# Gated mix of two linear attentions: query factors over one denominator, per-bank copies and earlier loads for the third query pair

## The chip, the cores and the metric

The kernel runs on one core of a Trainium2 chip. The metric is the device time of one execution in microseconds (us). The engines are PE (TensorE, the matmuls; PEld is its weight loader), DVE (VectorE), ACT (ScalarE), POOL (GpSimd) and SP (SyncE, which issues the DMA transfers; SPq is its queue).

## The reference

Two linear attentions over the same 2048 rows of 576 features, with 32 heads of 18 features, are mixed by a gate.

```python
g = _sigmoid((x * gate_w).sum(-1, keepdims=True))
a = _A_ref(x, A_wqkv, A_wo)      # phi = elu-like map of q and k
b = _B_ref(x, B_wqkv, B_w_phi, B_wo)
return g * a + (1 - g) * b
# inside B, per head, q and k first times w_phi:
phi_q = concatenate([softmax(pq), softmax(-pq)])      # 36 features from 18
kv = einsum("bhsf,bhsd->bhfd", phi_k, v);  z = sum over s of phi_k
o = (phi_q @ kv) / (phi_q @ z + 1e-6)
```

The part that matters here is B's query side. With u0 = exp(pq - max) and u1 = exp(min - pq), s0 and s1 their sums over the 18 features of a head, and z0, z1 the two halves of z, the two halves of phi_q are u0/s0 and u1/s1, and the denominator is u0.z0/s0 + u1.z1/s1 + 1e-6. Every row and head thus needs two factors, f0 = (1-g)/(s0 * den) for u0 and f1 = (1-g)/(s1 * den) for u1.

## The kernel before, in words

Rows go in 16 tiles of 128, two at a time: eight pairs. Three passes over the pairs follow each other: A's keys and values, B's keys and values, then the queries of both. Products with the weights are one level of Strassen on 2x2 blocks (`strassen`, lines 549 to 590): seven products per pair, accumulated in PSUM. Every float32 value is split into a high and a low float32r part, and three matmuls make up one product.

The query pass is `q_units` (lines 1169 to 1197) for a pair's Strassen steps. Its accumulators are X, Y and Z. X is filled with the first product, copied into SBUF as c1 (`keep`, line 556, on ACT), then more products are added into the same X: s2 (copied as c2), s3 (copied as c3), and the product of block 22, which is read as it stands. So PE cannot begin the next product into X before ACT has copied the last. Y is added to c1 on DVE (line 570), which also sets free the buffer that Z takes. X, Y and Z are two-bank PSUM tiles (`pq_tile`, tag pq, two buffers), with 288 columns in each bank, except that X of the first two pairs is made of two separate one-bank tiles (tags tr and bk, line 1192), which are copied one by one. `softmax_exp` (line 689) makes u0 and u1 (buffers named uw; vo and st stand for them in the second pair), their sums `ss` and, with one DVE reciprocal of 128x64, `rs`. `norm_a` (line 1127) and `norm_b` (line 1148) then make the scaled features: `norm_b` multiplies u by z_b (zw, one of the two on POOL), reduces to `dd` (128x64), multiplies dd by rs on POOL, adds the two halves and EPS to `den`, takes its reciprocal on DVE, and forms the factors in rs (line 1160); `scale_ub` writes u times its factor into the block buffer `late` (on POOL for the first two pairs, on DVE later). `tr_units` (line 1199) transposes A's features (`tr<-ident,row`) and the scaled blocks (`tr<-ident,late`) on PE, and ACT copies them out as uT. `num` (line 1220) multiplies uT with kb, the folded key-value blocks of B, and its results (vo, at) are copied by ACT and split by DVE. `out_units` (line 1244) multiplies them with the output weights WO (`bk<-op,vo`, `bk<-op,at`, `bk<-tail,at`) and stores the rows.

`fold_b` (line 1102) writes z_b and, by twelve small transfers on SP's queue (line 1124, 36 partitions of two or three runs of 18 numbers), kb. `x_fetch` (line 528) issues a pair's seven loads: xu, x1, xv, x2 (t2), then xp (s2 and s1), x3 (s3), x4 (s4, d), most of them into single buffers that the pair before still reads. The third query pair (n == 2 in `q_units`) has its loads issued in the loop's turn i == 1 (line 1302).

What sets the order of the work: the program is first recorded as a list of operations (`Plan`), each with its engine, its cost by a small formula and a due time worked backwards from the operations that need it (`order`, line 240); `run` (line 277) then picks, engine by engine, the ready operation that is due first. The order of each engine is so fixed when the program is built. All instructions carry the line of the call in `emit` (360; 365 in the changed kernel), so in the profile they are told apart by the names of their tiles.

## Time and profile before

| | us |
|---|---|
| median of 3 runs (lowest, highest) | 545.13 (544.47, 549.06) |
| the profiled execution, its own time | 544.94 |
| its span, first to last instruction | 543.2 |
| PE busy | 537.2 |
| DVE, ACT, POOL busy | 408.2, 291.1, 256.4 |
| granted TensorE clock | 0.999 |

How to read it: a row of the timeline gives the start in us, the duration of the group in us (first start to last end), engine, operation, out<-in, shapes, and how often; in brackets stands the idle time before it and what ended that. Matmul ends are modelled, so a group of matmuls seems to overlap the next: the pace is read from the starts of groups that follow each other. PEld's gaps show a wait of PE more fully than PE's own, for the same reason. A row of the windows view gives, for a stretch, the busy time of each engine, then the granted clock, the DMA share and GB/s.

### The profile page before, as it was taken

How to read it: one execution, taken by the hardware profiler on the slowest of the kernel's cores; microseconds unless marked ns; L12 is line 12 of the kernel's file. 1: busy time of each engine (PE TensorE's matmuls, PEld its weight loads, DVE VectorE, ACT ScalarE, POOL GpSimd, SP SyncE). 2: the span in 40 equal slices, each digit the busy share in tenths (PEclk: the TensorE clock that was granted, in tenths of full speed). 3: DMA queues.
4: the chain of work that ended last, by engine and by line, in shares of the span. 5: the costliest groups of instructions: out<-in, count | busy, mean ns of one | idle time of the engine just before them, and what ended most of it. 6: DMA issues, size and time to landing. Idle time of an engine off the chain costs nothing.

```text
span 543.2 us, 12968 instructions
## 1 busy us (share of the span) xinstructions
PE 537.2 (99%) x5233; PEld 518.6 (95%) x5233; DVE 408.2 (75%) x610; ACT 291.1 (54%) x612; POOL 256.4 (47%) x238
## 2 busy tenths in 40 slices
PE   9999999999999999999999999999999999999997
PEld 8999999999999999999999799999999999999997
DVE  5885587852798899989779989569598695976910
ACT  6865786645555645543376665354453544635430
POOL 5785486541884534363348685134252342523300
PEclk9999999999999999999999999999999999999999
DMA  8838767967759768768774831132231322200101
GB/s 288 321 127 268 270 242 273 344 219 305 277 220 339 250 201 280 237 210 261 290 268 147 347 98 59 57 116 71 81 101 59 110 72 81 70 24 1 45 23 43
DMA packets 40404, 96.38 MB, mean 177 GB/s; under 512 B 5460, under 2 KB 10068, under 8 KB 38808
## 3 DMA queue, kind: packets, MB, share of 16 engines
q1 hardware_dynamic: 40344, 95.56, 50.8%
q8 instruction: 41, 0.67, 0.5%
q14 instruction: 19, 0.16, 0.1%
HBM read 59.64 MB, written 36.70 MB: 177 GB/s over the span
## 4 chain that ended last, share of the span: by engine, by line
PE 96%; DMA 3%; DVE 0%; SPq 0%; issue 0%
PE pq L360 39%; PE bk L360 28%; PE tr L360 28%; DMA op<-wod 2%; DMA x<-s1x 1%; DVE row L360 0%; DVE dd L360 0%; SPq L360 0%; DVE epsc L360 0%
## 5 line engine op out<-in xcount | busy, mean ns | idle before, releaser
L360 PE MATMUL pq<-op,x 128*128 128x288 f32 (+1 forms) x624 | 102.3, 298 | 0.7 <-ACT row L360 0.7
L360 PEld LDWEIGHTS pq<-op,x 128*128 128x128 f32 x624 | 88.8, 188 | 1.5 <-ACT row L360 1.0
L360 PE MATMUL bk<-op,vo 128*128 128x288 f32 x480 | 70.7, 296 | 0.0
L360 PE MATMUL pq<-tail,x 128*128 128x288 f32 (+1 forms) x304 | 66.8, 299 | 0.3 <-DVE row L360 0.3
L360 PEld LDWEIGHTS bk<-op,vo 128*128 128x128 f32 x480 | 65.8, 188 | 0.0
L360 POOL TENSOR_TENSOR row<-row,z_a 128x576 f32<-128x576 f32 x16 | 25.8, 1609 | 60.1 <-issue 35.7
L360 PE MATMUL pq<-op,xp 128*128 128x288 f32 (+1 forms) x336 | 53.6, 297 | 0.1
L360 PE MATMUL bk<-op,at 128*128 128x288 f32 x288 | 51.0, 302 | 0.0
L360 PEld LDWEIGHTS pq<-tail,x 128*128 128x128 f32 x304 | 49.0, 188 | 1.5 <-issue 0.6
L360 POOL TENSOR_TENSOR row<-row,den 128x378 f32<-128x378 f32 (+1 forms) x32 | 23.8, 763 | 53.0 <-DVE den L360 53.0
L360 PEld LDWEIGHTS pq<-op,xp 128*128 128x128 f32 x336 | 47.4, 189 | 0.4 <-ACT row L360 0.4
L360 ACT ACTIVATE uT<-tr 118x512 f32<-118x512 f32 (+1 forms) x48 | 26.4, 561 | 39.1 <-PE tr L360 39.1
L360 ACT ACTIVATE row<-tr 128x288 f32<-128x288 f32 (+1 forms) x74 | 30.1, 408 | 29.8 <-PE tr L360 28.7
L360 ACT ACTIVATE row<-row,epsc 128x576 f32<-128x576 f32 x54 | 41.8, 774 | 3.3 <-DVE row L360 2.7
L360 PEld LDWEIGHTS bk<-op,at 128*128 128x128 f32 x288 | 41.5, 189 | 0.4 <-issue 0.4
L360 DVE TENSOR_REDUCE ss<-uw 128x64 f32<-128x1152 f32 x22 | 29.6, 1347 | 14.3 <-ACT uw L360 14.3
L360 POOL TENSOR_TENSOR x<-at,x 128x384 fp32r<-128x384 f32 (+2 forms) x35 | 32.0, 918 | 16.8 <-ACT x L360 14.9
L360 DVE TENSOR_TENSOR row<-row,pq 128x576 f32<-128x576 f32 (+1 forms) x30 | 22.2, 739 | 22.2 <-ACT row L360 15.5
L360 ACT ACTIVATE row<-bk 128x288 f32<-128x288 f32 (+2 forms) x42 | 17.2, 410 | 35.5 <-PE bk L360 35.3
L360 PE MATMUL tr<-op,xp 128*128 128x290 f32 (+1 forms) x216 | 33.4, 298 | 0.0
L360 ACT ACTIVATE uw<-uw 128x1152 f32<-128x1152 f32 x22 | 25.6, 1165 | 11.0 <-POOL uw L360 6.9
L360 PEld LDWEIGHTS tr<-op,xp 128*128 128x128 f32 x216 | 30.3, 189 | 0.2
(214 smaller groups left out, 1253.1 us busy)
## 6 DMA issues: line engine op xcount, KB each, us to landing
xp<-s0x SPq DMA_DIRECT2D x12, 512.0 KB
at<-xT SPq DMA_DIRECT2D x16, 320.0 KB
x<-x1x SPq DMA_DIRECT2D x12, 384.0 KB
x<-s2x SPq DMA_DIRECT2D x12, 384.0 KB
s0x<-xp SPq DMA_DIRECT2D x8, 512.0 KB
out<-row SPq DMA_DIRECT2D x14, 288.0 KB
op<-wb SPq DMA_DIRECT2D x3, 1152.0 KB
wod<-op SPq DMA_DIRECT2D x3, 1152.0 KB
```

The costliest lines, as they stand in the source:

```text
L360: fn(*[a.real() if isinstance(a, View) else a for a in args], **{k: v.real() if isinstance(v, View) else v for k, v in kw.items()})
```

## The change

There are three edits, and the planner's new order that follows from them.

1. B's query factors. For queries, `softmax_exp` returns the sums ss and takes no reciprocal of them. The factors are written over one denominator: with d0 = u0.z0 and d1 = u1.z1, f0 = (1-g) * s1 / (d0*s1 + d1*s0) and f1 = (1-g) * s0 / (d0*s1 + d1*s0). `norm_b` so multiplies dd on POOL by ss with its two halves swapped, adds the halves, takes the one reciprocal of 128x32, and forms the factors in dd. The 1e-6 has moved into z_b, as half of it per feature in each half (a bias of the ACT copy in `fold_b`). Sixteen DVE reciprocals of 128x64 go away, two per pair.
2. The third pair's X and Z are two-bank tiles that the planner tracks by bank: ACT copies c1, c2 and c3 in two instructions of 288 columns instead of one of 576, and the adds of Z are made in two.
3. The due times of the third pair's loads are set 15 us earlier (`plan.head = 15000`), so that the planner puts them between the transfers into kb.

```diff
     def cells(self):
 
         if self.tile.psum:
-            return np.zeros(1, np.int32)
+            return np.unique(self.idx[0] // 512).astype(np.int32) if self.tile.split else np.zeros(1, np.int32)
         if self.tile.dram:
             return self.idx.reshape(-1)
         n = math.prod(self.tile.shape[1:])
...
             op = Op()
             op.i, op.eng, op.calls, op.deps, op.succ, op.tiles = len(self.ops), eng, [], set(), [], set()
             op.cost, op.lag, op.lock, op.mode, op.dma = 0, 0, False, False, 0
+            op.head = self.head
             self.ops.append(op)
             if self.group is not None:
                 self.group.append(op)
...
             if op.eng != "PE":
                 after = [ops[s].due for s in (*op.succ, *frees.get(op.i, ()))]
                 op.due = min(after + [op.due + 60000]) - op.cost - op.lag - self.SEM
+        for op in ops:
+            if op.eng != "PE":
+                op.due -= op.head
         return self.run(tags)
 
     def run(self, tags):
...
     def tr_tile():
         return ps.tile([P, 512], F32, name="tr")
 
+    def halves_tile():
+        t = pq_tile()
+        t.tile.split = True
+        return t
+
     def two_banks(make=None):
         return [(make or tr_tile)() for _ in range(2)]
 
...
         if isinstance(acc, View):
             return [(slice(0, 2), acc)]
         return [(slice(a, a + 1), t[:, None]) for a, t in enumerate(acc)]
+
+    def by_half(acc):
+        return isinstance(acc, View) and acc.tile.split
 
     def half(acc, hf):
         return acc[:, hf] if isinstance(acc, View) else acc[hf]
...
     def tail_steps(x, w):
         return [(x(0, 0), w), (x(1, 0), w)]
 
-    def strassen(x, W, T, n, x_tile, c1_tile, c11, c22, c21, c12):
+    def strassen(x, W, T, n, x_tile, c1_tile, c11, c22, c21, c12, z_tile=pq_tile):
 
 
         def mul(acc, steps, start):
...
                 mm(acc, hf, n, steps, start, True)
 
         def keep(dst, acc, w):
+            if by_half(acc):
+                for a in range(2):
+                    A.activation(dst[:, a], acc[:, a, :w], AF.Copy)
+                return
             for a, t in parts(acc):
                 A.activation(dst[:, a], t[:, :, :w], AF.Copy)
 
...
         c2 = row_tile()[:, :D].rearrange("p (a c) -> p a c", a=2)
         keep(c2, X, HB)
         yield
-        Z = pq_tile()
+        Z = z_tile()
         mul(Z, tail_steps(x["t2"], T[:, 1]) + op_steps(x["s1"], W[5]), True)
         yield
         mul(X, op_steps(x["s3"], W[7]), False)
...
             V.scalar_tensor_tensor(fv[:, a], t[:, :, :HB], EPS, fv[:, a], op0=ALU.max, op1=ALU.add)
         return f
 
-    def softmax_exp(q, uw, eng=V):
+    def softmax_exp(q, uw, eng=V, inv=True):
         mm_ = sm.tile([P, 64], F32, name="mm")
         V.tensor_reduce(mm_[:, :32], heads(q), op=ALU.max, axis=AX.X)
         V.tensor_reduce(mm_[:, 32:], heads(q), op=ALU.min, axis=AX.X)
...
         A.activation(uw, uw, AF.Exp)
         ss = sm.tile([P, 64], F32, name="ss")
         V.tensor_reduce(ss, uw.rearrange("p s (h d) -> p (s h) d", d=DH), op=ALU.add, axis=AX.X)
+        if not inv:
+            return uw, ss
         rs = sm.tile([P, 64], F32, name="rs")
         V.reciprocal(rs, ss)
         return uw, rs
...
             pz = bank_tile()
             PE.matmul(pz[:, :36 * nh], sel[:, q], KB[:, :36 * nh], start=True, stop=True)
             A.activation(z_b[:, :, QH * DH * q:QH * DH * q + DH * nh].rearrange("p s (j d) -> p j s d", d=DH),
-                         pz[:, :36 * nh].rearrange("p (j s d) -> p j s d", s=2, d=DH), AF.Copy)
+                         pz[:, :36 * nh].rearrange("p (j s d) -> p j s d", s=2, d=DH), AF.Copy, bias=EPS / 2)
         pt = bank_tile()
         for m in range(3):
             PE.transpose(pt[:108, P * m:P * m + P], KB[:, 108 * m:108 * m + 108], ident)
...
         A.activation(ub[:, UB * 10 + 72:UB * NB], f2[:, 484:530], AF.Copy)
         return f2
 
-    def norm_b(t, uw, rs, ub, engs):
+    def norm_b(t, uw, ss, ub, engs):
         dd = sm.tile([P, 64], F32, name="dd")
         for s in range(2):
             zw = row_tile()[:, :D]
             engs[s].tensor_tensor(zw, uw[:, s, :], z_b[:, s], op=ALU.mult)
             V.tensor_reduce(dd[:, 32 * s:32 * s + 32], zw.rearrange("p (h d) -> p h d", d=DH),
                             op=ALU.add, axis=AX.X)
-        G.tensor_tensor(dd, dd, rs, op=ALU.mult)
+        swap = ss.rearrange("p (s h) -> p s h", s=2)[:, ::-1]
+        d2 = dd.rearrange("p (s h) -> p s h", s=2)
+        G.tensor_tensor(d2, d2, swap, op=ALU.mult)
         den = sm.tile([P, 32], F32, name="den")
-        V.scalar_tensor_tensor(den, dd[:, :32], EPS, dd[:, 32:], op0=ALU.add, op1=ALU.add)
+        V.tensor_tensor(den, dd[:, :32], dd[:, 32:], op=ALU.add)
         V.reciprocal(den, den)
-        r2 = rs.rearrange("p (s h) -> p s h", s=2)
-        V.scalar_tensor_tensor(r2, den[:, None, :].to_broadcast([P, 2, 32]), gate[:, 1, at_row(t):at_row(t) + 1], r2, op0=ALU.mult, op1=ALU.mult)
-        scale_ub(ub, uw, rs, engs[2])
+        V.scalar_tensor_tensor(d2, den[:, None, :].to_broadcast([P, 2, 32]), gate[:, 1, at_row(t):at_row(t) + 1], swap, op0=ALU.mult, op1=ALU.mult)
+        scale_ub(ub, uw, dd, engs[2])
 
     qs, norms = {}, []
     pairs = [NT // 2 - 2, NT // 2 - 1, *range(NT // 2 - 2)]
...
         qa, qb = {}, {}
 
         def c11(c):
-            qb[t1] = softmax_exp(c, uws[0], G)
+            qb[t1] = softmax_exp(c, uws[0], G, False)
+
+        def add(c, Z):
+            for a in ([slice(a, a + 1) for a in range(2)] if by_half(Z) else [slice(0, 2)]):
+                V.tensor_tensor(c[:, a], c[:, a], Z[:, a, :HB], op=ALU.add)
 
         def c22(c, Z):
-            V.tensor_tensor(c, c, Z[:, :, :HB], op=ALU.add)
+            add(c, Z)
             qa[t2] = phi_elu(c)
 
         def c21(X):
-            qb[t2] = softmax_exp(whole(X, uws[1]), uws[1])
+            qb[t2] = softmax_exp(whole(X, uws[1]), uws[1], V, False)
 
         def c12(c, Z):
-            V.tensor_tensor(c, c, Z[:, :, :HB], op=ALU.add)
+            add(c, Z)
             qa[t1] = phi_elu(c)
 
         def norm(t):
...
             qs[t] = (norm_a(t, qa[t], ub), ub)
             norm_b(t, *qb[t], ub, (G, V, G if t < 4 else V))
 
-        x_tile = (two_banks, lambda: two_banks(bank_tile))[n] if n < 2 else pq_tile
-        for i, _ in enumerate(strassen(x, WQ, TQ, HB, x_tile, c1_tile, c11, c22, c21, c12)):
+        x_tile = (two_banks, lambda: two_banks(bank_tile))[n] if n < 2 else halves_tile if n == 2 else pq_tile
+        for i, _ in enumerate(strassen(x, WQ, TQ, HB, x_tile, c1_tile, c11, c22, c21, c12, halves_tile if n == 2 else pq_tile)):
             if i in then:
                 then[i]()
             yield
...
         if i and i <= NT // 2:
             prev["ot"] = num(uT, prev["at"], i >= NT // 2 - 1)
         if i + 1 < NT // 2:
+            plan.head = 15000 if i == 1 else 0
             x = x_fetch(pairs[i + 1])
+            plan.head = 0
             if i == 0:
                 load_out(3, x["dma"])
                 load_out(4, x["dma"])
```

`cells` decides what the planner takes for one place in a tile; the lines left out only declare the new fields.

Where instructions move, first on SP, at the transfers into kb (the names x_ with a number are loads into x1, x2, x3 and x4). Before:

```order
L360 DMA kb<-row 36x3x18 x2
L360 DMA kb<-row 36x2x18
L360 DMA xu<-x0x_181 128x512
L360 DMA xp<-s0x_1972 128x1024
L360 DMA x_4206<-s1x_1992 128x512
L360 DMA op<-mad 2x2x1152
L360 DMA tail<-mad 2x1152
L360 DMA op<-wod 128x2304
L360 DMA xv<-x2x_231 128x512
```

and now, with the rows of the first two kb transfers ahead of it the same:

```order
L365 DMA xu<-x0x_181 128x512
L365 DMA kb<-row 36x2x18
L365 DMA kb<-row 36x3x18 x2
L365 DMA kb<-row 36x2x18
L365 DMA kb<-row 36x3x18
L365 DMA xp<-s0x_1972 128x1024
L365 DMA kb<-row 36x3x18
L365 DMA kb<-row 36x2x18
L365 DMA x_4167<-s1x_1992 128x512
L365 DMA kb<-row 36x3x18 x2
L365 DMA kb<-row 36x2x18
L365 DMA xv<-x2x_231 128x512
```

Three of the third pair's loads (xu, xp and s1x) now stand between the kb transfers, and xv ahead of the loads of the output weights.

On POOL, at the two `norm_b` of the first pair, from the first dd to the subtractions of the second pair's softmax (vo is that pair's u). Before:

```order
L360 TENSOR_TENSOR dd<-dd,rs 128x64
L360 TENSOR_TENSOR late<-uw,rs 128x10x3x18 x2
L360 TENSOR_TENSOR late<-uw,rs 128x2x2x18
L360 TENSOR_TENSOR dd<-dd,rs 128x64
L360 TENSOR_TENSOR row<-row,den 128x3x126
L360 TENSOR_TENSOR row<-row,den 128x198
L360 TENSOR_TENSOR late<-uw,rs 128x10x3x18 x2
L360 TENSOR_TENSOR late<-uw,rs 128x2x2x18
L360 TENSOR_TENSOR vo<-mm,row 128x576
L360 TENSOR_TENSOR vo<-row,mm 128x576
```

and now:

```order
L365 TENSOR_TENSOR dd<-dd,ss 128x64
L365 TENSOR_TENSOR late<-uw,dd 128x10x3x18 x2
L365 TENSOR_TENSOR late<-uw,dd 128x2x2x18
L365 TENSOR_TENSOR dd<-dd,ss 128x64
L365 TENSOR_TENSOR row<-row,den 128x3x126
L365 TENSOR_TENSOR row<-row,den 128x198
L365 TENSOR_TENSOR vo<-mm,row 128x576
L365 TENSOR_TENSOR late<-uw,dd 128x10x3x18 x2
L365 TENSOR_TENSOR late<-uw,dd 128x2x2x18
L365 TENSOR_TENSOR row<-row,z_a 128x576
L365 TENSOR_TENSOR vo<-row,mm 128x576
```

The subtraction vo<-mm,row now stands ahead of the second group of late, and the product with z_a ahead of the other subtraction.

On PE, at the third pair's X: s2 is `pq<-op,xp x12`, s3 the `pq<-op,x x12` behind it, block 22 `pq<-op,xv`; Z begins with `pq<-tail,x`. Before:

```order
L360 MATMUL bk<-op,at 128x288 x6
L360 MATMUL bk<-tail,at 128x288 x3
L360 MATMUL bk<-op,vo 128x288 x2
L360 MATMUL pq<-op,xp 128x288 x12
L360 MATMUL pq<-op,x_4206 128x288 x12
L360 MATMUL pq<-tail,x_3962 128x288 x2
L360 MATMUL pq<-op,xp 128x288 x6
L360 MATMUL pq<-tail,x_3962 128x288 x2
L360 MATMUL pq<-op,xp 128x288 x6
```

and now:

```order
L365 MATMUL pq<-op,x_4045 128x288 x6
L365 MATMUL pq<-tail,x_4045 128x288 x2
L365 MATMUL bk<-op,vo 128x288 x2
L365 MATMUL pq<-op,xp 128x288 x12
L365 MATMUL pq<-op,x_4167 128x288 x12
L365 MATMUL pq<-op,xv 128x288
L365 MATMUL pq<-tail,x_3962 128x288 x2
L365 MATMUL pq<-op,xp 128x288 x6
L365 MATMUL pq<-tail,x_3962 128x288 x2
L365 MATMUL pq<-op,xp 128x288 x6
L365 MATMUL pq<-op,xv 128x288 x5
```

One matmul of block 22 has moved ahead of Z, and the output product with at (six and three) is no longer there: it stands some 40 matmuls earlier, between the first product into X and the first group of late.

On DVE, what leads up to the addition of Y to c1, which is `row<-row,pq 128x576` here. Before:

```order
L360 RECIPROCAL rs<-ss 128x64
L360 SCALAR_TENSOR_TENSOR row<-row 128x576
L360 RECIPROCAL den<-den 128x32
L360 TENSOR_REDUCE ss<-st 128x64
L360 TENSOR_REDUCE dd<-row 128x32
L360 RECIPROCAL rs<-ss 128x64
L360 TENSOR_TENSOR at<-bk,at 64x256
L360 TENSOR_TENSOR row<-vo,z_b 128x576
L360 TENSOR_REDUCE dd<-row 128x32 x2
L360 TENSOR_TENSOR row<-row,pq 128x576
L360 TENSOR_TENSOR row<-st,z_b 128x576
```

and now:

```order
L365 TENSOR_REDUCE den<-row 128x32
L365 TENSOR_TENSOR row<-st,z_b 128x576
L365 TENSOR_REDUCE dd<-row 128x32
L365 RECIPROCAL den<-den 128x32
L365 TENSOR_REDUCE ss<-vo 128x64
L365 TENSOR_REDUCE dd<-row 128x32
L365 TENSOR_REDUCE ss<-st 128x64
L365 TENSOR_TENSOR row<-vo,z_b 128x576
L365 TENSOR_REDUCE dd<-row 128x32 x2
L365 TENSOR_TENSOR row<-row,pq 128x576
L365 TENSOR_TENSOR den<-dd 128x32
L365 RECIPROCAL den<-den 128x32
```

The two reciprocals of ss are gone, the product of st with z_b has moved from behind the addition to the head of the list, and at<-bk and the row<-row of phi have moved away from it.

More of the change, by code (lines that the diff above doesn't have):

```diff
@@ L118, in __init__ @@
         self.ops = 0
+        self.split = False
     def view(self):
@@ L136 @@
 class Op:
-    __slots__ = ("i", "eng", "calls", "deps", "succ", "tiles", "cost", "lag", "lock", "mode", "dma", "due", "left", "est", "key")
+    __slots__ = ("i", "eng", "calls", "deps", "succ", "tiles", "cost", "lag", "lock", "mode", "dma", "head", "due", "left", "est", "key")
 class Engine:
@@ L151, in __init__ @@
     def __init__(self):
-        self.ops, self.tiles, self.group, self.first = [], [], None, ()
+        self.ops, self.tiles, self.group, self.first, self.head = [], [], None, (), 0
     @contextmanager
```

## The prediction

> **What bounds the kernel now.** I read the page's busy times first, then PE's idle time by stretches, then the weight loader's timeline where it lies.
>
> ```profile
> span 543.2 us, 12968 instructions
> ...
> PE 537.2 (99%) x5233; PEld 518.6 (95%) x5233; DVE 408.2 (75%) x610; ACT 291.1 (54%) x612; POOL 256.4 (47%) x238
> ```
>
> PE is busy for all but 6.0 us, and the change takes no matmul away, so it can only win idle time of PE. The windows view (the stretch, its length, then busy us of PE, PEld, DVE, ACT and POOL) shows where that is:
>
> ```profile
> 0.00:295.00 295.00, 293.75 (x3369) 286.52 (x3370) 229.47 (x314) 175.91 (x374) 160.66 (x147) 1.00 0.74 255
> 295.00:315.00 20.00, 18.51 (x137) 16.33 (x135) 19.23 (x30) 12.06 (x24) 14.91 (x16) 1.00 0.84 324
> 315.00:520.00 205.00, 205.00 (x1583) 197.34 (x1582) 157.12 (x263) 99.44 (x207) 80.83 (x77) 1.00 0.21 68
> 520.00:543.20 23.20, 19.94 (x151) 18.43 (x150) 2.40 (x5) 3.72 (x9) 0.00 (x0) 0.99 0.11 39
> ```
>
> 1.25 us are the start and 3.26 us the last copy and store; neither is touched. The other 1.5 us lie between 295 and 315 us, where the second query pair ends and the third begins and DVE is busy for 19.23 of 20 us. From 315 us on PE waits for nobody: what is won before stays won, and DVE time saved later is worth nothing. Since PE's ends are modelled, the weight loader shows the waits more fully:
>
> ```profile
> 295.86 0.69 PEld L360 LDWEIGHTS pq<-op,xu 128*128 128x128 f32 x5 [0.52 <-DVE mm L360]
> ...
> 305.56 1.62 PEld L360 LDWEIGHTS pq<-op,xp 128*128 128x128 f32 x12 [0.36 <-ACT row L360]
> 308.16 1.62 PEld L360 LDWEIGHTS pq<-op,x 128*128 128x128 f32 x12 [0.97 <-ACT row L360]
> 310.32 0.30 PEld L360 LDWEIGHTS pq<-tail,x 128*128 128x128 f32 x2 [0.54 <-DVE row L360]
> ```
>
> Four waits, 0.52 + 0.36 + 0.97 + 0.54 = 2.4 us: the most that the change can win. That is 0.44%, under the 1% that a measurement of this kernel can tell from no change.
>
> The chain of waits puts the last of them down to a load, which is wrong:
>
> ```profile
> 294.02 5.71 DMA x<-s1x
> ...
> 300.17 8.65 DMA op<-wod
> ...
> 308.87 0.74 DVE dd L360
> ```
>
> The reduction at 308.87 is the second of two on a DVE that never paused (rows below); the weights only happen to land 0.05 us earlier. DVE's own queue sets that wait.
>
> **Part by part: the first wait.** The loader's row blames DVE, but PE's own row says that it was the load of xu:
>
> ```profile
> 282.69 10.21 SPq L360 DMA_DIRECT2D kb<-row  x12
> 293.00 0.46 SPq L360 DMA_DIRECT2D xu<-x0x  x1
> ```
>
> ```profile
> 282.04 1.86 PE L360 MATMUL bk<-op,xu 128*128 128x288 f32 x12
> ...
> 295.89 0.90 PE L360 MATMUL pq<-op,xu 128*128 128x288 f32 x5 [0.31 <-DMA xu<-x0x]
> ...
> 299.65 1.95 PE L360 MATMUL tr<-uT,kb 118*64 118x256 f32 x16
> ...
> 303.82 0.95 PE L360 MATMUL bk<-op,at 128*128 128x288 f32 x6
> 304.61 0.56 PE L360 MATMUL bk<-tail,at 128*128 128x288 f32 x3
> ```
>
> The kb issues take 0.85 us each on SP; xu goes out behind all twelve and is used 2.9 us later. Now it stands behind two, at about 282.7 + 1.7 = 284.4, and lands near 287.3; its buffer's last read by the second pair, the group from 282.04, is over by then. So the 0.5 us go, and PE begins the third pair at 295.4. The three loads put between push the last kb issue from about 292.1 to 293.3, or 294 if xp waits a little for PE. PE first reads kb at 299.65, which covers this: even if a kb transfer took the 5.7 us of s1x above, it would land just in time.
>
> **The second wait.** The first product's X has to be copied as c1 before s2 goes into it. ACT comes to that late; from the last uT copy on its queue is full:
>
> ```profile
> 298.87 0.49 ACT L360 ACTIVATE uT<-tr 118x384 f32<-118x384 f32 x1
> 299.24 1.17 ACT L360 ACTIVATE vo<-vo 128x1152 f32<-128x1152 f32 x1
> ...
> 304.87 0.64 ACT L360 ACTIVATE row<-pq 128x576 f32<-128x576 f32 x1
> 307.45 0.65 ACT L360 ACTIVATE row<-pq 128x576 f32<-128x576 f32 x1 [1.94 <-PE pq L360]
> 308.70 0.21 ACT L360 ACTIVATE row<-row 128x6 f32<-128x6 f32 x1 [0.60 <-POOL row L360]
> ```
>
> 299.24 to 305.51 is 6.3 us of work without a pause. The new order has the same ACT work between uT and c1, so the question is when that uT copy is made. It hangs on the second group of late, which POOL writes:
>
> ```profile
> 289.15 2.57 POOL L360 TENSOR_TENSOR late<-uw,rs 128x540 f32<-128x540 f32 x3 [1.50 <-DVE rs L360]
> ...
> 292.00 1.31 POOL L360 TENSOR_TENSOR row<-row,den 128x378 f32<-128x378 f32 x2
> 293.67 2.56 POOL L360 TENSOR_TENSOR late<-uw,rs 128x540 f32<-128x540 f32 x3 [0.36 <-DVE rs L360]
> 296.18 1.17 POOL L360 TENSOR_TENSOR vo<-mm,row 128x576 f32<-128x576 f32 x1
> ```
>
> Now vo<-mm,row is ahead of that group. The first group starts about 0.2 later (DVE has moved a dd and the split of at ahead of its factors, but lost two reciprocals), so POOL reaches vo<-mm,row at 293.5, and 293.5 + 1.17 + 2.56 gives 297.2: 1.0 us later than 296.2. PE meanwhile does 12 matmuls on xu and four of the output product: 295.4 + 16 x 0.132 = 297.5 (0.132 us from the six at 303.82). It just does not wait. Eleven transposes and five matmuls later, about 299.5, the last uT copy can start; it ends at 300.1. ACT's 6.3 us, less the second bank's share of 0.6, put the first bank of c1 at 305.8. So **s2 starts at 305.8 instead of 305.56**: what the early load won is lost again in ACT's queue, and this wait grows to about 1.2.
>
> **The split's own price**, from the groups of this pass:
>
> ```profile
> L360 ACT ACTIVATE row<-bk 128x288 f32<-128x288 f32 x33 | 13.5, 408 | 23.2 <-PE bk L360 23.1
> ...
> L360 ACT ACTIVATE row<-pq 128x576 f32<-128x576 f32 x18 | 11.7, 651 | 14.6 <-PE pq L360 14.6
> ```
>
> 2 x 408 against 651 ns: +0.17 us, three times, 0.5 on an ACT that sits idle for 0.6 and 1.9 us beside the copies of c2 and c3. Z's two added DVE instructions come behind the point that counts.
>
> **The third wait.** Whole, c2 is copied from 307.45 on, when both banks are done, and s3 waits until 308.16. By bank, s2's first half ends at 305.8 + 0.8 and 0.3 for the pipeline (307.45 against the 307.15 that 305.56 + 1.6 gives), and its copy ends at 307.3, while PE does the second half until 307.4. ACT has the row<-row of 308.70 and two late copies ahead of it, 0.6 us, which wait for POOL until about 306.2 (four products behind the exponential of st, below: 301.9 + 1.4 + 0.8 + 1.4 + 0.6 by POOL's rows for the same); that ends near 307.2. So **s3 starts at 307.4 instead of 308.16, a net 0.75**.
>
> **The fourth wait.** Z takes Y's buffer when DVE has added Y to c1 (the row at 309.53):
>
> ```profile
> 300.44 1.35 DVE L360 TENSOR_REDUCE ss<-vo 128x64 f32<-128x1152 f32 x1 [0.68 <-ACT vo L360]
> ...
> 303.04 0.55 DVE L360 RECIPROCAL rs<-ss 128x64 f32<-128x64 f32 x1
> 303.50 0.70 DVE L360 SCALAR_TENSOR_TENSOR row<-row 128x576 f32<-128x576 f32 x1
> ...
> 306.23 0.54 DVE L360 RECIPROCAL rs<-ss 128x64 f32<-128x64 f32 x1
> 306.69 0.35 DVE L360 TENSOR_TENSOR at<-bk,at 64x256 fp32r<-64x256 f32 x1
> 306.97 1.32 DVE L360 TENSOR_TENSOR row<-vo,z_b 128x576 f32<-128x576 f32 x1
> 308.21 1.40 DVE L360 TENSOR_REDUCE dd<-row 128x32 f32<-128x576 f32 x2
> 309.53 0.74 DVE L360 TENSOR_TENSOR row<-row,pq 128x576 f32<-128x576 f32 x1
> ```
>
> 303.04 to the start of the next instruction, 310.19, is 7.15 us. The two reciprocals go (2 x 0.46 by the distance of starts), row<-row (0.6) and at<-bk (0.3) have moved away; row<-st,z_b (0.7), one more dd (0.65) and ss<-vo (1.27) have moved in: 7.9 us. It would be 7.4 if row<-vo,z_b ran at its 0.7 instead of 1.24, without POOL beside it. The new list begins with row<-st,z_b, which needs the exponential of st: that is the second item of ACT's queue after 300.1, behind one of 0.7, so done at 301.9. The addition ends at 309.3 to 309.8 against 310.19. PE has finished s3 and one more matmul at 309.15 and waits again, 0.3 to 0.8. Z starts at 309.45 to 310.0 with one matmul (0.13) more behind it: a gain of 0.45 to 1.0 us. **I take 0.8**, since POOL's product with vo has moved forward and meets DVE's less.
>
> Behind that, the subtraction of vo on DVE, which PE's next transposes need, is by the same sums 0.3 us ahead of PE. The other twelve reciprocals go from turns in which PE waits for nothing. The 1e-6 in the z_b copies, the swapped halves and tensor_tensor for scalar_tensor_tensor replace instructions one for one: nothing.
>
> The sum, against the profiled execution: 544.94 - 0.8 = **544.1 us**. That execution lies 0.2 under the median of the runs shown, well inside their spread, so the forecast stays.
>
> **The rivals.**
>
> *All of the wait goes* (0.17): 544.94 - 2.4 = 542.5. For it: each wait has an edit aimed at it. Against it: ACT would have to reach c1 1.2 us, and DVE the addition 1.5 us, before the times above.
>
> *Nothing moves* (0.20): if a matmul into the first bank waits for both copies after all, s3 starts at 308.1, and with DVE at its late end 0 to 0.4 are left: 544.5 to 544.9. Against it: the first two pairs keep X in two tiles, and no wait of PE shows at their s3.
>
> *Slower, from POOL* (0.15). The place is the second group of late, only 0.3 ahead of PE. The 297.2 uses undisturbed durations; beside DVE the same shape of instruction takes longer:
>
> ```profile
> 414.90 1.64 POOL L360 TENSOR_TENSOR uw<-mm,row 128x576 f32<-128x576 f32 x1
> ```
>
> 1.64 against the 1.17 of vo<-mm,row is 0.5 us. Two or three such stretches put the end of late at 298.2 to 298.7; then PE, uT, ACT's exponentials and DVE's list follow it one for one. From 298.0 the 0.8 is eaten; at 298.7, with row<-vo,z_b slow as well, the time is 545.6. Against it: DVE is in reductions for half of that time. The Trainium skill (SBUF — State Buffer, "Who interferes with whom") says that a DVE instruction with two SBUF inputs contends with a GpSimd instruction that reads SBUF, and that a reduction never does. The two durations agree with it. By that rule vo<-mm,row would not be stretched where it now stands, beside reductions, and the time would be the forecast's 544.1.
>
> **How the numbers follow.** The forecast has 0.48. All four cases lie between 542.5 and 545.6, inside the 1% (539.7 to 550.6), so same has 0.96; 0.02 on either side are for a wait in the later turns, which would count several times. The range takes both end cases in, with a little for the spread of a median: 542.4 to 546.0.
>
> **What would show it.** Right: PE at the first pq<-op,xu without a wait, near 295.4; s2's wait for ACT grown from 0.36 to about 1.2, s3's under 0.2; Z still waiting for DVE, 0.3 to 0.8; no wait from 315 on. Wrong: s2 starting before 305.3, s3 still waiting 0.5, or the second late holding PE up. A time outside the range would mean that a queue which I took to be covered decides.

## The result, and the profile after

| | before | after |
|---|---|---|
| median (lowest to highest), 21 runs each | 545.14 us (544.25 to 549.06) | 548.62 us (547.12 to 552.89) |
| ratio of the medians, 95% interval | | 1.0065 (1.0051 to 1.0079) |
| profiled execution, span | 544.94 us, 543.2 us | 549.28 us, 547.5 us |

The changed kernel is 3.5 us slower; 544.1 had been forecast, with 546.0 as the upper end. The prediction took 1% for the least that a measurement of this kernel can tell from no change; the interval here tells 0.65%. The page of the execution after, and its windows view (the same stretches as before; length, then busy us of PE, PEld, DVE, ACT and POOL):

```profile
span 547.5 us, 12948 instructions
...
PE 537.8 (98%) x5233; PEld 518.8 (95%) x5233; DVE 400.6 (73%) x596; ACT 291.4 (53%) x615; POOL 259.6 (47%) x238
```

```profile
0.00:295.00 295.00, 292.79 (x3358) 285.43 (x3359) 227.74 (x309) 174.93 (x370) 159.86 (x146) 1.00 0.74 257
295.00:315.00 20.00, 16.34 (x121) 14.15 (x120) 16.49 (x25) 11.45 (x28) 15.07 (x14) 1.00 0.68 259
315.00:520.00 205.00, 204.38 (x1575) 196.48 (x1575) 153.32 (x256) 99.84 (x206) 84.66 (x80) 1.00 0.21 71
```

DVE does 7.6 us less, as the removed reciprocals should, and PE does the same matmuls. The time is lost where the three edits lie: PE is idle for 3.66 us between 295 and 315 us instead of 1.49, and for 0.62 us behind 315, where it had not waited at all. Another 0.96 us, ahead of 295, is not the change's: in this execution PE waited at 175 us for a load of wqT, ahead of every changed instruction. The same wait is 0, 0.56 or 1.13 us long in profiles of the kernels below, with the same instructions up to there. With smaller differences ahead of it, the execution after reaches the second pair's last product on xu 1.33 us later than the one before (283.37 against 282.04); times of the two are compared less that.

The weight loader's timeline shows each wait of the stage:

```profile
296.62 1.64 PEld L365 LDWEIGHTS pq<-op,xu 128*128 128x128 f32 x12
299.74 0.56 PEld L365 LDWEIGHTS bk<-op,at 128*128 128x128 f32 x4 [1.49 <-DMA op<-mad]
...
308.79 1.62 PEld L365 LDWEIGHTS pq<-op,xp 128*128 128x128 f32 x12 [1.33 <-ACT row L365]
311.45 1.36 PEld L365 LDWEIGHTS pq<-op,x 128*128 128x128 f32 x10 [1.03 <-ACT row L365]
313.54 0.30 PEld L365 LDWEIGHTS pq<-op,x 128*128 128x128 f32 x2 [0.73 <-ACT row L365]
...
316.41 0.56 PEld L365 LDWEIGHTS pq<-op,xp 128*128 128x128 f32 x4 [0.85 <-DVE row L365]
```

The wait at xu is gone. In its place stand a wait for a load ahead of the output product (1.49), a longer one ahead of s2 (1.33 for 0.36), the old one ahead of s3 (1.03 for 0.97), and two that the kernel before does not have at all, in the middle of a product: s3 stops after 10 of its 12 matmuls (0.73), Z after the second of its last six (0.85). Together 5.43 us for 2.39, which is 3.04 more and, to a few tenths, the whole loss.

ACT's timeline shows why the stops are there. Its copies of X, in the order c1, c2, and the two banks of c3, and then DVE's addition of Z's first bank:

```profile
308.05 0.70 ACT L365 ACTIVATE row<-pq 128x288 f32<-128x288 f32 x2
...
310.69 0.71 ACT L365 ACTIVATE row<-pq 128x288 f32<-128x288 f32 x2 [0.76 <-PE pq L365]
313.08 0.41 ACT L365 ACTIVATE row<-pq 128x288 f32<-128x288 f32 x1 [1.68 <-PE pq L365]
314.24 0.41 ACT L365 ACTIVATE row<-pq 128x288 f32<-128x288 f32 x1 [0.75 <-PE pq L365]
```

```profile
315.90 0.46 DVE L365 TENSOR_TENSOR row<-row,pq 128x288 f32<-128x288 f32 x1 [1.68 <-PE pq L365]
```

s2 ran from 308.79 to 310.41, its first bank to 309.6. The copy of that bank starts at 310.69, when both banks are done, though ACT had been idle for 0.76. The copy of the first bank of c3 starts at 313.08, when PE has done four matmuls into the second bank, and PE's next matmul into the second bank waits for that copy. The stop inside Z is of the same kind: the addition of its first bank stands between matmuls into its second, and PE goes on at 316.41, when the addition is done. In the instruction list this is what the semaphores say: the copy of bank 0 of c2 waits for the count that the sixth matmul into bank 1 raises, the first matmul of s2, into bank 0, waits for the count that the copy of bank 1 of c1 raises, and the eleventh matmul of s3, into bank 1, waits for the count that the copy of bank 0 raises. The planner keeps two places for the tile, the semaphores one.

That PE and ACT can work on two banks at the same time is seen in the kernel before, in the second pair, whose X is two separate tiles. Its first copy of c2, then the second half of its s2:

```profile
286.88 0.41 ACT L360 ACTIVATE row<-bk 128x288 f32<-128x288 f32 x1 [0.46 <-PE bk L360]
```

```profile
287.00 0.84 PEld L360 LDWEIGHTS bk<-op,xp 128*128 128x128 f32 x6
```

The copy waits for the first bank alone and runs while PE fills the second, and PE goes on into s3 at 287.78 without a wait.

### The profile page after: what moved, and what is told of

It is laid out like the page before. It is cut to its first block, busy times and chain, and to the rows that moved or that the text cites. A ratio compares the mean times of both kernels' runs of the same rounds, so it can differ in the third digit from the quotient of the medians.

```text
span 547.5 us, 12948 instructions
## 1 busy us (share of the span) xinstructions
PE 537.8 (98%) x5233; PEld 518.8 (95%) x5233; DVE 400.6 (73%) x596; ACT 291.4 (53%) x615; POOL 259.6 (47%) x238
## 4 chain that ended last, share of the span: by engine, by line
PE 96%; DMA 2%; ACT 1%; DVE 0%; issue 0%; SPq 0%; ACTq 0%; DVEq 0%
PE pq L365 40%; PE bk L365 28%; PE tr L365 28%; DMA at<-wqT 1%; ACT row L365 1%; DMA op<-mad 1%; ACT vo L365 0%; DVE row L365 0%; ACT st L365 0%; ACT den L365 0%; ACT at L365 0%; SPq L365 0%; ACTq L365 0%; ACT uT L365 0%; DVE epsc L365 0%
## 5 line engine op out<-in xcount | busy, mean ns | idle before, releaser
L365 POOL TENSOR_TENSOR row<-row,den 128x378 f32<-128x378 f32 (+1 forms) x32 | 22.0, 708 | 53.5 <-DVE den L365 53.3
L365 DVE TENSOR_TENSOR row<-row,pq 128x576 f32<-128x576 f32 (+2 forms) x32 | 22.4, 702 | 27.8 <-ACT row L365 21.0
L365 PE MATMUL tr<-op,x 128*128 128x288 f32 (+1 forms) x204 | 30.4, 297 | 0.0
```

The source lines that it names most:

```text
L365: fn(*[a.real() if isinstance(a, View) else a for a in args], **{k: v.real() if isinstance(v, View) else v for k, v in kw.items()})
```

## The experiments

The theory after the result had two parts. **The bank split** fails since the semaphores guard the two-bank tile as one: it cannot start the copy earlier, and where the planner, believing otherwise, puts a read of one bank between matmuls into the other, PE stops. **The order**: the edits make the planner move the output product ahead of its small weights op<-mad. The rivals were the first edit's instructions themselves, POOL's contention from the prediction, and the early loads. Each edit was run by itself first, then the parts of the order. Each kernel was timed beside the kernel before on the same chip.

**e_factors: the first edit alone.**

```diff
-        x_tile = (two_banks, lambda: two_banks(bank_tile))[n] if n < 2 else halves_tile if n == 2 else pq_tile
+        x_tile = (two_banks, lambda: two_banks(bank_tile))[n] if n < 2 else pq_tile
...
-            plan.head = 15000 if i == 1 else 0
```

(against the changed kernel; `z_tile` is pq_tile too.)

> The first edit alone: one denominator for B's query factors, without the copies by bank and with the loads of the third pair behind kb as before. If the slowdown comes from the copies by bank and from the late op<-mad, this kernel is at 544.6 to 545.6, no different from before, with 0.3 to 0.5 us of wait at xu back, s3 stopped once and never in the middle of a product. If the new chain of factors is what costs (the rival, POOL's product with the sums between DVE's reductions), it is at 547 to 549.

547.11 us (546.65 to 548.57); ratio to before 1.0028 (1.0008 to 1.0048). Slower: the theory as it stood had this at 544.6 to 545.6 and was wrong. The loader's waits:

```profile
303.27 0.63 PEld L365 LDWEIGHTS tr<-uT,kb 118*64 118x64 f32 x8 [0.24 <-ACT uT L365]
...
306.65 1.63 PEld L365 LDWEIGHTS pq<-op,xp 128*128 128x128 f32 x12 [1.22 <-ACT row L365]
309.77 0.30 PEld L365 LDWEIGHTS pq<-tail,x 128*128 128x128 f32 x2 [1.49 <-DVE row L365]
...
314.49 0.43 PEld L365 LDWEIGHTS pq<-op,xv 128*128 128x128 f32 x3 [0.97 <-ACT row L365]
```

Removing the reciprocals has changed the order on every engine: POOL now makes vo<-row,mm before the second group of late, PE does Z (which waits for DVE) ahead of s3, and DVE's two subtractions into st stand beside POOL's products. Rows of POOL, then of DVE, then of ACT:

```profile
294.92 3.08 POOL L365 TENSOR_TENSOR late<-uw,dd 128x540 f32<-128x540 f32 x3 [0.16 <-DVE dd L365]
297.96 1.42 POOL L365 TENSOR_TENSOR row<-row,z_a 128x576 f32<-128x576 f32 x1
299.34 1.68 POOL L365 TENSOR_TENSOR vo<-mm,row 128x576 f32<-128x576 f32 x1
```

```profile
298.36 1.64 DVE L365 TENSOR_TENSOR st<-mm,st 128x576 f32<-128x576 f32 x1
300.03 1.61 DVE L365 TENSOR_TENSOR st<-st,mm 128x576 f32<-128x576 f32 x1
```

```profile
301.67 1.17 ACT L365 ACTIVATE st<-st 128x1152 f32<-128x1152 f32 x1 [1.10 <-DVE st L365]
302.74 0.47 ACT L365 ACTIVATE uT<-tr 118x384 f32<-118x384 f32 x1
```

ACT waits for the stretched st, and the last uT copy, which the numerator's product needs, stands behind it. From there the copy of c1 and s2 are late.

**e_banks: the second edit alone**, on the kernel before: `cells`, `halves_tile`, the copies and additions by bank as in the diff of the change, nothing else.

> The second edit alone: X and Z of the third pair read by bank, everything else as before. Theory: the semaphores take the two banks as one tile, so that a copy of the first bank waits for the last matmul into the second and a matmul into the second bank waits for the copy of the first; then PE stops in the middle of s2, s3 or Z, two or three times for 0.6 to 0.9 us, the wait ahead of s3 stays near 0.9, and the time is 546.3 to 547.6. Rival: the copies by bank work as the prediction had it and the loss is elsewhere; then the wait ahead of s3 is under 0.2 and the time 544.2 to 545.2.

546.98 us (546.17 to 549.91); 1.0035 (1.0010 to 1.0059). The time and the stops are as the theory had them; the 0.9 that it expected ahead of s3 is not there:

```profile
298.74 0.19 PEld L365 LDWEIGHTS bk<-op,at 128*128 128x128 f32 x1 [0.99 <-DMA op<-mad]
...
306.62 1.37 PEld L365 LDWEIGHTS pq<-op,xp 128*128 128x128 f32 x10 [0.56 <-ACT row L365]
308.71 0.30 PEld L365 LDWEIGHTS pq<-op,xp 128*128 128x128 f32 x2 [0.73 <-ACT row L365]
308.96 0.46 PEld L365 LDWEIGHTS pq<-op,x 128*128 128x128 f32 x3
310.14 0.43 PEld L365 LDWEIGHTS pq<-op,x 128*128 128x128 f32 x3 [0.73 <-ACT row L365]
...
314.74 0.30 PEld L365 LDWEIGHTS pq<-op,xv 128*128 128x128 f32 x2 [0.73 <-ACT row L365]
```

Three products stop in the middle, each for 0.73. That s3 starts without a wait (308.96) helps nothing: the 0.97 has been cut into 0.73 inside s2 and 0.73 inside s3. And the wait for op<-mad is here without the early loads, since the planner has moved the output product forward here too.

**e_early: the third edit alone**, on the kernel before: `head` and the two lines that set it.

> The third edit alone: the loads of the third pair between the transfers into kb. The output product stands here behind all of Y, so its late weights op<-mad have 2.5 us more; theory: no wait for op<-mad, the 0.5 us at xu gone, the rest as before, 544.4 to 545.2. If the early loads cost by themselves, because the transfers behind them come late (kb or op<-mad), a wait for a DMA of 0.5 us or more stands between 297 and 304 us and the time is 545.8 to 547.

545.05 us (543.55 to 547.44); 0.9984 (0.9960 to 1.0008). PE takes up xu without a wait, and every later wait is that of the kernel before to 0.01 us:

```profile
295.66 0.70 PEld L365 LDWEIGHTS pq<-op,xu 128*128 128x128 f32 x5
...
305.38 1.62 PEld L365 LDWEIGHTS pq<-op,xp 128*128 128x128 f32 x12 [0.35 <-ACT row L365]
307.98 1.62 PEld L365 LDWEIGHTS pq<-op,x 128*128 128x128 f32 x12 [0.97 <-ACT row L365]
310.14 0.30 PEld L365 LDWEIGHTS pq<-tail,x 128*128 128x128 f32 x2 [0.54 <-DVE row L365]
```

A gain of 0.5 in the trace; in the times too little to tell from none. This edit moves nothing but SP's rows.

**e_fe: the first and the third edit.** `halves_tile` is not used; the rest is the changed kernel.

> The first and the third edit, without the copies by bank. The output product stands behind all of Y here too. Theory: no wait for op<-mad and no stop in the middle of a product, 544.2 to 545.2, at most 0.8 faster than before; with the changed kernel at 548.6 the copies by bank, directly and by the order that they bring, then carry 3.4 to 4 us. Rival, that the factors and the early loads together delay ACT and DVE: 546.5 to 548, with s2 or Z waiting over 1 us.

547.53 us (546.85 to 551.20); 1.0037 (1.0012 to 1.0063). The rival's case: the waits are those of e_factors, with 1.22 ahead of s2 and 1.51 ahead of Z, and what the early xu wins there (0.68) comes back as a longer wait for uT (0.96 for 0.24). So the loss is not the bank split alone; the first edit brings about as much by itself.

**fac_order: the first edit in the old order.** The planner is given a step that issues nothing, with the cost of a reciprocal, in place of each one removed. The order of PE, ACT, POOL and SP is then that of the kernel before, row for row.

```diff
         if not inv:
+            plan.add("DVE", lambda *a, **k: None, "reciprocal", (ss,), {"in_": ss[:, :]})
             return uw, ss
```

> The first edit alone, but placed by the planner as if the sixteen removed reciprocals still stood on DVE with their old cost (nothing is issued for them): the order of PE, ACT, POOL and SP is that of the kernel before, row for row, and DVE's is too but for the missing reciprocals. If the first edit costs by the order that it brings, this kernel is not slower than before: 544.3 to 545.3, the wait of Z for DVE (0.54) down to under 0.2, s2 and s3 waiting 0.3 to 0.4 and 0.9 to 1.0 as before. If the new instructions cost by themselves (the rival), it is at 546.5 to 547.5 like the first edit alone.

544.80 us (543.90 to 546.08); 0.9991 (0.9979 to 1.0003). Not slower: the new instructions cost nothing that shows, and the order that they bring costs what e_factors lost, 2.0 us by the two ratios. Z's wait falls from 0.54 to 0.24 (under 0.2 was expected):

```profile
306.99 1.63 PEld L365 LDWEIGHTS pq<-op,xp 128*128 128x128 f32 x12 [0.36 <-ACT row L365]
309.59 1.61 PEld L365 LDWEIGHTS pq<-op,x 128*128 128x128 f32 x12 [0.97 <-ACT row L365]
311.44 0.30 PEld L365 LDWEIGHTS pq<-tail,x 128*128 128x128 f32 x2 [0.24 <-DVE row L365]
```

**fe_order: the first and the third edit in that order** (the added step, and `head`).

> The first and the third edit with the reciprocals kept in the planner's books: the order of the kernel before, with the loads of the third pair between those into kb. If order is the whole price, the gains that the prediction gave to these two edits come out: no wait at xu (0.5) and Z's wait under 0.2 (another 0.3 to 0.5), so 544.0 to 544.8 and the only large wait left is the 0.9 to 1.0 ahead of s3. If the two edits cost beside the order, 546 to 548.

544.51 us (543.34 to 547.72); 0.9991 (0.9975 to 1.0008). No wait at xu, 0.34 ahead of s2, 0.97 ahead of s3, 0.24 ahead of Z (under 0.2 was expected). By the two ratios this is 2.5 us less than the same two edits in the planner's own order.

**banks_order: the second edit in the old order.** Each pair of by-bank instructions is one step for the planner, at the old cost, and `cells` takes the tile as one place. No read stands between the matmuls of a product.

```diff
-                for a in range(2):
-                    A.activation(dst[:, a], acc[:, a, :w], AF.Copy)
+                with plan.piece():
+                    for a in range(2):
+                        A.activation(dst[:, a], acc[:, a, :w], AF.Copy)
+                plan.ops[-1].cost -= 62
```

> The second edit alone: the copies of c1, c2, c3 and the additions of Z made by bank, each pair of instructions one step for the planner at the old cost, so that the order of all engines is that of the kernel before. Here no copy is put between matmuls of one product. If the semaphores take the two banks as one tile, the first copy of c2 still starts only when both halves of s2 are done, s3 waits 0.95 to 1.1 as before, and the time is 545.0 to 545.6. If they go by bank (the rival), the first copy starts when PE is in the second half, s3 waits under 0.4 and the time is 544.3 to 544.9.

545.64 us (544.21 to 546.93); 0.9994 (0.9971 to 1.0017), no difference. Whether a copy by bank can start earlier is seen in ACT's row for c2 and the loader's for s2 and s3:

```profile
306.98 0.71 ACT L365 ACTIVATE row<-pq 128x288 f32<-128x288 f32 x2 [1.95 <-PE pq L365]
```

```profile
305.08 1.62 PEld L365 LDWEIGHTS pq<-op,xp 128*128 128x128 f32 x12 [0.42 <-ACT row L365]
307.74 1.62 PEld L365 LDWEIGHTS pq<-op,x 128*128 128x128 f32 x12 [1.04 <-ACT row L365]
```

It cannot. The first bank was complete at about 305.9, ACT waited for PE for 1.95 us all the same and began at 306.98, 0.3 behind the second bank, as with one copy. s3 waits 1.04 for 0.97, the 0.07 being what two copies take longer (0.71 for 0.65).

**mad_early: the changed kernel with op<-mad earlier.** The two small pieces of op<-mad and tail<-mad are issued from behind the fourth transfer into kb on; no other engine's order changes. For tail<-mad the same line is added, and `head` is set back to 0 behind it.

```diff
+            plan.head = 20000
             SP.dma_start(to[126:], MA_d[570:574].rearrange("(g p) s n -> p g s n", g=2))
```

> The changed kernel, only with the two small pieces of op<-mad and tail<-mad issued behind the fourth transfer into kb instead of behind the twelfth; PE's order is unchanged. If the 1.49 us at the first matmul of the output product is the late piece, that wait is gone or under 0.2 and the time is 546.9 to 547.7. If something else holds PE there too (the second group of late, which PE needs five matmuls later), the wait moves to the transposes of late, 0.5 to 1.0 comes back, and the time is 547.7 to 548.4. If the wait was one execution's chance, 548.4 to 549.

546.78 us (545.81 to 549.60); 1.0024 (1.0002 to 1.0045), 0.1 under what was expected. The wait is gone and comes back nowhere, not at the transposes of late either:

```profile
296.24 0.59 PEld L365 LDWEIGHTS bk<-op,at 128*128 128x128 f32 x4
296.77 0.92 PEld L365 LDWEIGHTS tr<-ident,late 128*118 128x118 f32 x8
...
305.34 1.62 PEld L365 LDWEIGHTS pq<-op,xp 128*128 128x128 f32 x12 [1.20 <-ACT row L365]
```

The ratios of the changed kernel and of this one differ by 0.41%, 2.2 us with intervals of 0.8 and 1.2 on either side; the trace gives 1.6. The late piece was real, and the largest single wait of the changed kernel.

**whole_plan: the changed kernel with `cells` as before**, so that the planner takes the two banks as one place again while the instructions stay by bank.

```diff
-            return np.unique(self.idx[0] // 512).astype(np.int32) if self.tile.split else np.zeros(1, np.int32)
+            return np.zeros(1, np.int32)
```

> The changed kernel with one line back: the planner again takes the two banks of X and Z as one tile, while copies and additions stay by bank, so that the planner puts no read of a bank between the matmuls of a product. Theory: the stops inside s3 (0.73) and inside Z (0.85) go, the wait for op<-mad (1.49) and s2's (1.3) stay: 546.7 to 547.5. Rival, that PE waits for ACT and DVE there whatever the planner believes: the same 1.6 us turn up ahead of s3 or Z and the time stays at 548.2 to 549.

548.02 us (547.11 to 550.66); 1.0051 (1.0033 to 1.0069). Between the theory's number and the rival's. The two stops are gone, but

```profile
309.23 0.96 PEld L365 LDWEIGHTS pq<-op,x 128*128 128x128 f32 x7 [1.03 <-ACT row L365]
...
312.27 0.71 PEld L365 LDWEIGHTS pq<-op,x 128*128 128x128 f32 x5
314.02 0.70 PEld L365 LDWEIGHTS pq<-op,xv 128*128 128x128 f32 x5 [1.04 <-ACT row L365]
```

the planner now puts Z between the seventh and the eighth matmul of s3, and block 22 behind s3 waits for the copy of c3 with nothing to cover it. In the kernel before, Z's 16 matmuls cover that copy. The waits add up to 5.10 us (with one of 0.19 behind block 22) for 5.43, so only 0.3 of the 1.58 is won (0.8 by the two ratios, whose intervals overlap). That the rest lies in how the order covers the copies of X is read from this trace, not tested by itself.

**fac_pool: the first edit with one decision turned back.** An added dependency makes POOL's two subtractions into vo wait for the second group of late.

```diff
+        plan.first = wait[1:]
         eng.tensor_tensor(v4(1), bc2(mm_[:, 32:]), heads(q), op=ALU.subtract)
```

> The first edit alone with one decision of the planner turned back by an added dependency: POOL makes the second group of late before the two products into vo (the softmax of the second pair), as in the kernel before; the rest of the order is the planner's own. If this one decision is what the first edit costs (late, then uT, then the numerator's product, then the copy of c1), the time is 544.8 to 545.8. If the other moves count as well (DVE's subtractions of st beside POOL, Z ahead of s3), it is at 546.2 to 547.1.

545.90 us (545.09 to 547.65); 1.0011 (0.9997 to 1.0026). Between the two cases: by the medians about half of the first edit's loss is gone, though the interval overlaps that of e_factors. Here s2 does not wait for c1 at all, but s3 and block 22 still wait 0.97 and 0.98. Which of the other moves brings the remaining half was not taken apart further.

**all_order: all three edits in the old order**, with the additions of fac_order and banks_order.

> All three edits of the changed kernel, with the removed reciprocals kept in the planner's books and each pair of by-bank instructions one step at the old cost: the order of the kernel before, with the loads of the third pair between those into kb. If the whole loss of the changed kernel is the order, this one is 3.5 to 4.5 us faster than it, at 544.2 to 545.0, with waits of 0.4 at s2, 1.05 at s3 and under 0.2 at Z and none at xu or in the middle of a product. If any of the edits costs beside the order, it is at 545.5 or above.

544.46 us (543.70 to 547.49); 0.9984 (0.9966 to 1.0001).

```profile
295.70 0.70 PEld L365 LDWEIGHTS pq<-op,xu 128*128 128x128 f32 x5
...
305.48 1.62 PEld L365 LDWEIGHTS pq<-op,xp 128*128 128x128 f32 x12 [0.42 <-ACT row L365]
308.14 1.62 PEld L365 LDWEIGHTS pq<-op,x 128*128 128x128 f32 x12 [1.03 <-ACT row L365]
```

Two waits are left, 1.45 us for the 2.39 before; Z no longer waits. By the two ratios this is 0.8% or 4.4 us less than the changed kernel, which issues the same work in another order (596 instructions on DVE, 615 on ACT and 238 on POOL in both): **the whole loss is order.** Its median is also the lowest of all, some 0.9 us under the kernel before, but its interval reaches 1, and e_early has the same ratio: a gain over the kernel before is seen in the trace and not shown by the times.

The waits of the stage side by side, in us, from the loader's timelines (0.2 and less left out; "inside" is in the middle of a product; e_factors and e_fe also wait 0.24 and 0.96 for uT, and 0.39 each for vo):

| kernel | xu | op<-mad | s2 | s3 | Z | 22 | inside | median |
|---|---|---|---|---|---|---|---|---|
| before | 0.52 | | 0.36 | 0.97 | 0.54 | | | 545.1 to 545.3 |
| after | | 1.49 | 1.33 | 1.03 | | | 0.73 + 0.85 | 548.62 |
| e_factors | 0.68 | | 1.22 | | 1.49 | 0.97 | | 547.11 |
| e_banks | 0.76 | 0.99 | 0.56 | | | | 3 x 0.73 | 546.98 |
| e_early | | | 0.35 | 0.97 | 0.54 | | | 545.05 |
| e_fe | | | 1.22 | | 1.51 | 0.97 | | 547.53 |
| fac_order | 0.71 | | 0.36 | 0.97 | 0.24 | | | 544.80 |
| mad_early | | | 1.20 | 1.03 | | | 0.73 + 0.85 | 546.78 |
| whole_plan | | 1.52 | 1.32 | 1.03 | | 1.04 | | 548.02 |
| fac_pool | 0.88 | | | 0.97 | | 0.98 | | 545.90 |
| banks_order | 0.32 | | 0.42 | 1.04 | 0.42 | | | 545.64 |
| fe_order | | | 0.34 | 0.97 | 0.24 | | | 544.51 |
| all_order | | | 0.42 | 1.03 | | | | 544.46 |

## Why the prediction was wrong, by its own steps

**The first wait: right.** PE takes up xu without a wait, at 296.62, which less the 1.33 is 295.3 (295.4 forecast), and kb is in time. e_early gives the 0.5 by itself.

**The second wait: its size right, its beginning wrong.** The wait ahead of s2 came out at 1.33 for about 1.2, but s2 starts at 308.79, which less the 1.33 is 307.5, not at 305.8. What failed is the step that led there, "PE meanwhile does 12 matmuls on xu and four of the output product" and "just does not wait". The order had moved the output product forward, and the prediction followed the late transposes behind it without asking when the product's own weights land. The chain of waits after has the load:

```profile
296.73 2.96 DMA op<-mad
```

It lands at 299.69, and PE stands from 298.26 to 299.74. In the kernel before it was issued at 294.46 and used at 303.82, so that it showed in no view as something close. e_banks shows the wait (0.99) without the early loads: the price is of the product's moving, not of SP's queue. With the load early, in mad_early, the rest of the step comes out: s2 waits 1.20 and starts at 305.34, which is 305.9 on the clock of the kernel before (mad_early reaches the last product on xu 0.60 us earlier). It starts there behind both copies of c1, which end at 305.29, and not behind the first, as the prediction had it.

The second group of late was later than forecast:

```profile
296.21 3.08 POOL L365 TENSOR_TENSOR late<-uw,dd 128x540 f32<-128x540 f32 x3 [0.16 <-DVE dd L365]
```

It ends at 299.29, which less the 1.33 is 298.0, for the 297.2 forecast, but PE was already waiting for op<-mad and reaches it at 300.24. It would not have held PE up otherwise: in mad_early the group takes the same 3.08 us, and PE takes up the transposes without a wait.

**The third wait: the step that failed outright.** "By bank, s2's first half ends at 305.8 + 0.8 ... and its copy ends at 307.3, while PE does the second half": the copy starts behind both halves, in the changed kernel and in banks_order. The 0.75 that this wait was to win came out as a wait of 1.03 for the 0.97 before. The prediction took the planner's places for the guards of the program. Its rival "nothing moves" (0.20) came nearest to the mechanism, a guard on both banks together, but not to its worse side: with a planner that believes in two places, the order lets a copy into the middle of a product, and each costs 0.73 to 0.85. The argument against that rival, that the first two pairs show no wait at s3, was weak: they hold X in two tiles, which are guarded apart (the rows of 286.88 and 287.00 above).

The Trainium skill (PSUM — Partial Sum Buffer, "Summary: rules for kernel authors") advises to read another bank while a matmul runs and to guard by bank. The copy at 286.88, beside matmuls into the other bank from 287.00 on, agrees. The third pair's traces show what happens when the data are split by bank and the guards are not; a run with the third pair's X in two tiles was not made.

**The fourth wait: DVE's list right, its beginning wrong.** The list from row<-st,z_b to the end of Y's addition took 7.6 us, as forecast (7.4 to 7.9):

```profile
304.66 0.76 DVE L365 TENSOR_TENSOR row<-st,z_b 128x576 f32<-128x576 f32 x1 [2.20 <-ACT st L365]
...
311.50 0.74 DVE L365 TENSOR_TENSOR row<-row,pq 128x576 f32<-128x576 f32 x1
```

But it began at 304.66, which less the 1.33 is 303.3, for the 301.9 forecast: the exponential of st stands behind the uT copies, which were late with PE. The addition ends at 312.24, which less the 1.33 is 310.9, for the 309.3 to 309.8 forecast. Z does not wait for it all the same, since the waits ahead keep PE from Z until 313.91; the 0.85 inside Z is the addition of Z's own first bank, the second edit's price. That the two reciprocals shorten the wait is seen where the order is kept: from 0.54 to 0.24 in fac_order, and below 0.2 in all_order.

**The reciprocals and the order of the first edit.** "The other twelve reciprocals go from turns in which PE waits for nothing" holds: in fac_order too PE is busy for all 205.00 us from 315 to 520. What was missed is that removing a planned cost is a change of order for all engines. Much of it was in the comparison of orders, and the forecast worked out two of its consequences, on POOL and DVE, and took the rest as it came.

**The rival "slower, from POOL"** had the stretch (the second group of late 3.08 for 2.56, forecast as 0.5 per stretch), but a time of 545.6. In mad_early the stretch costs PE nothing; whether it is a part of e_factors' loss, where the group also takes 3.08, was not tested.

**The sum**: 0.8 was to be won. 0.94 is won in the trace when the order is kept (2.39 less 1.45), but that the two are near is chance: the 0.94 comes from xu and Z, and the 0.75 that the prediction had at s3 is not in it. In the changed kernel it went, and 3 us with it, to moves that the planner made on its own.

## What to carry to other kernels

A kernel whose order comes from a planner answers a removed instruction with another order; take the gain of the edit and the price of the order apart, by keeping the removed cost in the planner's books. Whenever an instruction moves forward, check every operand of it, the loads above all: one that was issued 9 us ahead of its use in the old order shows in no view as close. And splitting a read helps only if what guards the buffer is split too; otherwise nothing is won by it (banks_order), and the planner must go on treating it as one.

## What the runs showed of the hardware beside this

Two DVE subtractions with both inputs in SBUF took 1.64 and 1.61 us in e_factors (rows above). In the kernel before, the second of them took 0.75, while POOL had nothing to do (from 301.05 to 303.74):

```profile
301.71 0.75 DVE L360 TENSOR_TENSOR st<-st,mm 128x576 f32<-128x576 f32 x1
```

The ends in e_factors fit two engines that take turns by whole instructions rather than share a rate. POOL's row<-row,z_a, begun before them, ends at 299.38, and DVE's st<-mm,st ends 0.62 later, at 300.00; POOL's vo<-mm,row, begun at 299.34, ends 1.02 behind that, at 301.02; DVE's second subtraction ends 0.62 behind that, at 301.64. Each takes its turn, in about the time that it needs alone. The Trainium skill (SBUF — State Buffer, "Who interferes with whom") says that the two engines share one pair of ports under an exclusive lock, and that a DVE instruction with two SBUF inputs contends for it with a GpSimd instruction that reads SBUF; the trace agrees (1.64 and 1.61 for 0.75). The price of such a meeting is then what is left of the other's instruction, 0.9 us for DVE and 0.5 for POOL here, where the forecast had 0.5 for any.

The transfer of 18 KB into op<-mad took 2.96 us from issue to landing in the changed kernel, and in e_banks, with xu, xp and s1x issued in the 1.5 us ahead of it,

```profile
294.27 4.43 DMA op<-mad
```

half as much again.
